# First loads in another order, stores between stages and later loads of q and v on GpSimd's queue: attention and two feed-forward layers, fp32

## The chip, the core and the metric

One core of a Trainium2 chip. The metric is the device time in microseconds of one execution, the median of several runs. One further execution was taken with the hardware profiler; every row below is from that one.

## What is computed

Linear attention over 4 batches of 8 heads (576 rows, 64 columns each), then two feed-forward layers over 2304 tokens, 512 wide, 2048 hidden, fp32:

```
q_s = softmax(q, last axis);  k_s = softmax(k, over the rows)
kv  = k_s^T v;  x = q_s kv                     (per batch and head)
h   = x @ w_in;   x2  = (h * sigmoid(1.702 h)) @ w_out
h2  = x2 @ w_in2; out = (h2 * tanh(softplus(h2))) @ w_out2
```

The weights arrive as float64 and are read as pairs of 32-bit words.

## The kernel before

Every fp32 operand of a large product is split into a high and a low fp32r part, and a product is three matmuls: high by high, high by low, low by high. Tokens run in five blocks of 512, 512, 512, 384 and 384. For the first three, layer 1 is computed chunk by chunk of the hidden width (48 steps n): twelve matmuls of L959 (h = x w_in), the activation on ScalarE and VectorE, and, two steps later, twelve of L1028 into four accumulators. The tokens of the last two blocks go through layer 1, and all of layer 2 follows, in a Strassen form with seven products in place of eight (L1250, L1480, L1589).

Weights come in 32 tiles of 512 KB per layer. Each is loaded into one of four `raw` buffers, turned from float64 into fp32 by ScalarE (L398, L362) and VectorE (L409, L422, L366), and split into high and low (L352, L353, L345). Layer 1's tiles stay in SBUF as `wi` and `wo`; sums and differences of them for the Strassen form, and layer 2's, are computed along the way and stored to a DRAM area (`combos` for w_in, `outs` for w_out), from which later stages load them into `wi`. x2 between the layers goes through DRAM too (`x2d`), and the attention output of the last two blocks (`xd`). The stores come from `store` (L446, called by `keep` and `combine1`), `combine` (L528), `right_parts` (L1391), `x2_evac` (L1080), `x_part` (L871); the loads that read them back from `ring_load` and `x_load`.

Attention is computed block by block between the matmuls of layer 1. Block 0's q goes to `qr`, its k and v to `kt` and `vd` or `gt`, at the start of the program. For the later blocks `q_load` (L754) fills `qt` with four or eight loads per half, `v_load` (L581) fills `vt` with two loads per pair of heads, `k_load` (L568) fills `kt`. For block 1 these loads have no condition of their own except that their tile is free; for the blocks behind it they wait for a step of layer 1.

All operations are recorded first, and a planner (`Plan`, L20 to L190) orders them: a list scheduler that simulates each engine as a queue, with a cost for every operation. All DMAs are one engine, `DMA`, whose cost is size / 305 ns times a factor `slow`, at least 650 ns; it adds 1400 ns from an engine to a DMA and 1050 back. An elementwise operation recorded with `either` (L341) may go to VectorE or to GpSimd; `SPARE` is what the planner adds to the finish time of either before it compares them. The program is then written out in the planned order, so each engine runs its own operations in that order and waits on semaphores for the others. In the kernel before every DMA is issued by SyncE, in the planned order.

Of the kernel before, what the change touches and what calls it, by code (L numbers as in the profile page):

```python
# [19 lines left out]
class Plan:  # L20
# [6 lines left out]
    SPARE = {DVE: 700.0, POOL: 2000.0}  # L27
# [183 lines left out]
def tile_attention_moe_moe(  # L211
# [107 lines left out]
    def f32(t):  # L319
        return t.bitcast(F32)  # L320
# [13 lines left out]
    def dma(size, reads, writes, out, in_, slow=1):  # L334
        plan.op(
            [(DMA, max(size * slow / 305.0, 650.0), lambda: nc.sync.dma_start(out=out(), in_=in_()), False)],
            reads,
            writes,
        )
# [41 lines left out]
    def decoded(m, io, fc, ri, di, pace=[], signed=True):  # L381
# [10 lines left out]
        dma(P * 4096, pace, [rl, rh], lambda: dst, lambda: src)  # L392
# [53 lines left out]
    def store(n, keys, j, u, out, in_):  # L446
        dma(P * n * 4, keys, [("combo", j, u)], out, in_)
# [80 lines left out]
    def combine(j, keys):  # L528
# [21 lines left out]
        for u, (n, ri, src, keys) in enumerate(parts):  # L550
            t = raw[ri].bitcast(F32R)
            hk, lk = [("raw", ri, 0)], [("raw", ri, 1)]
            split(n, lambda t=t, n=n: t[:, 0:n], lambda t=t, n=n: t[:, n : 2 * n], src, keys, hk, lk)
            dma(
                P * n * 8,
                hk + lk,
                [("combo", NFC // 2 + j, u)],
                lambda u=u, n=n: combos[NFC // 2 + j][:, u * 1024 : u * 1024 + 2 * n],
                lambda t=t, n=n: f32(t[:, 0 : 2 * n]),
            )  # L560
# [7 lines left out]
    def k_load(u, begun):  # L568
# [6 lines left out]
            lambda: k[b, 2 * hp : 2 * hp + 2].rearrange("h (p c) d -> p h c d", c=KC),  # L575
        )
# [4 lines left out]
    def v_load(u, begun):  # L581
        b, hp = divmod(u, NHP)
        if b == 0:
# [5 lines left out]
                lambda: v[b, 2 * hp : 2 * hp + 2].rearrange("h (p c) d -> p h (c d)", c=KC),  # L589
            )  # L590
            return
        for j in range(2):
# [6 lines left out]
                slow=2,  # L599
            )  # L600
# [153 lines left out]
    def q_load(blk, half, begun):  # L754
        cuts = q_cuts(blk)
        for i, (lo, hi) in enumerate(cuts):
            b, s = divmod(BASE[blk] + lo, S)
            for j in range(4):
# [6 lines left out]
                    slow=2,  # L765
                )
        return q_keys(range(4))

    def q_soft(blk, half, begun):
# [5 lines left out]
        if blk == 0:  # L775
# [6 lines left out]
                lambda: q[0, 4 * half : 4 * half + 4, 0 : SIZES[0], :].rearrange("h (p c) d -> p h c d", c=NCT),  # L782
            )
# [87 lines left out]
    def x_part(blk, hp, ps, key, i):  # L871
# [11 lines left out]
        if blk >= NDIR:  # L883
            t, keys = stage[hp % 3][:, 0:nb], [("stage", hp % 3)]
            from_psum(n, lambda: part(t), part(ps[:, 0:nb]), [key], keys)
            if i == len(q_cuts(blk)) - 1:
                to = (blk - NDIR) * NB
                dma(P * nb * 4, keys, [("xd", blk, hp)], lambda: xd[:, hp, to : to + nb], lambda: t)
# [191 lines left out]
    def x2_evac(blk):  # L1080
# [4 lines left out]
        for dm in range(NCC):  # L1085
# [5 lines left out]
            dma(P * nb * 4, keys, [("x2d", blk, dm)], lambda dm=dm: x2d[:, dm, BASE[blk] : BASE[blk + 1]], t)  # L1091
# [299 lines left out]
    def right_parts(j, base, keys, signed):  # L1391
# [24 lines left out]
        dma(P * 2048, rk[1][:1], [("outs", 0, j, a) for a in range(2)], lambda: outs[0][:, j], lambda: halved(f32(two[:, 0:512])))  # L1416
        stores = [(1, a, f32(one[:, a * 512 : a * 512 + 512]), rk[0][a : a + 1]) for a in range(2)]
        stores += [(3, 0, f32(hi[0]), rk[1][1:]), (3, 1, a0, [d0, ("ob", 0, 1)]), (5, 0, f32(hi[1]), mk), (5, 1, a1, [d1, ("ob", 1, 1)])]
        for i, a, src, keys in stores:
# [6 lines left out]
                slow=1.3,  # L1426
            )
# [338 lines left out]
```

## Time and profile before

| | us |
|---|---|
| median of 3 runs | 821.22 (818.87 to 823.44) |
| the profiled execution's own time | 823.01 |
| its span, from the first to the last instruction | 821.2 |
| PE busy | 809.6 (99%) |
| VectorE busy | 659.4 (80%) |
| ScalarE busy | 455.8 (56%) |
| GpSimd busy | 17.3 (2%) |

207.7 MB move by DMA in that time, and the packets took 76.7% of 16 DMA engines' span. The busy share of PE is no measure of its pace, since matmuls are pipelined; what it waited for and the granted clock are read from rows.

### The profile page before, as it was taken

The page shows a single profiled execution, that of the slowest core. Times are in us where ns is not written, and L with a number is a line of the kernel's source. Part 1 is how long each engine was busy: PE and PEld are TensorE (multiplying, and loading weights), DVE is VectorE, ACT ScalarE, POOL GpSimd, SP SyncE. Part 2 cuts the span into 40 slices and gives each one's busy share as a digit, 9 for nine tenths or more (in the row PEclk, how much of TensorE's full clock was granted, in tenths as well). Part 3 has the DMA queues.
Part 4 walks back from the last instruction along what each step waited for, and adds up shares of the span by engine and source line. Part 5 has one row for each costly group of instructions (what it writes and reads, how often), then busy time and mean ns, then how long its engine had stood idle before and what let it go on. Part 6 is the DMA issues. An engine that isn't in the chain of part 4 may idle for free.

```text
span 821.2 us, 14388 instructions
## 1 busy us (share of the span) xinstructions
PE 809.6 (99%) x5102; PEld 735.8 (90%) x5102; DVE 659.4 (80%) x1277; ACT 455.8 (56%) x915; POOL 17.3 (2%) x22
## 2 busy tenths in 40 slices
PE   8999899999999999999999999999999999999998
PEld 7788677877778887999999999999999999999998
DVE  6999897888976689866789879978777969777964
ACT  5989675445765555745457644555344554344542
POOL 0000000000000000000000000000000005000000
PEclk9999899999999999999999999999999999999999
DMA  9789556555688699878878897979588887778862
GB/s 258 213 251 306 187 182 187 207 154 168 195 264 283 225 300 313 257 279 285 327 269 275 319 320 251 341 284 406 188 263 293 291 293 253 226 261 259 270 197 59
DMA packets 126983, 208.57 MB, mean 254 GB/s; under 512 B 37568, under 2 KB 87488, under 8 KB 126912
## 3 DMA queue, kind: packets, MB, share of 16 engines
q1 hardware_dynamic: 126912, 207.66, 76.7%
q8 instruction: 41, 0.67, 0.3%
q14 instruction: 30, 0.25, 0.1%
HBM read 152.57 MB, written 55.05 MB: 253 GB/s over the span
## 4 chain that ended last, share of the span: by engine, by line
PE 61%; DMA 2%; DVE 1%; ACT 0%; issue 0%; ACTq 0%; SPq 0%
PE acc L1480 22%; PE at L1250 18%; PE h L1250 10%; PE acc L1589 5%; PE h L1589 3%; PE acc L1028 2%; DMA raw<-in_moe_w_in_dram 1%; DMA combos<-raw 1%; PE h L959 1%; PE h L1480 0%; DVE raw L345 0%; PE at L878 0%; PE at L848 0%; DVE dec L345 0%; DVE dec L422 0%
## 5 line engine op out<-in xcount | busy, mean ns | idle before, releaser
L959 PE MATMUL h<-xt,wi 128*128 128x512 f32 x576 | 149.0, 402 | 0.2 <-DVE xt L838 0.2
L1028 PE MATMUL acc<-g,wo 128*128 128x512 f32 x576 | 147.5, 398 | 0.0
L1480 PE MATMUL acc<-wi,second 128*128 128x256 f32 x1116 | 137.5, 283 | 0.0
L1480 PEld LDWEIGHTS acc<-wi,second 128*128 128x128 f32 x1116 | 135.6, 192 | 0.0
L959 PEld LDWEIGHTS h<-xt,wi 128*128 128x128 f32 x576 | 107.4, 190 | 25.0 <-issue 1.5
L1028 PEld LDWEIGHTS acc<-g,wo 128*128 128x128 f32 x576 | 106.6, 189 | 22.7 <-issue 0.4
L1250 PE MATMUL at<-xt,wi 128*128 128x384 f32 x612 | 119.0, 335 | 0.1
L1250 PEld LDWEIGHTS at<-xt,wi 128*128 128x128 f32 x612 | 106.8, 188 | 2.8 <-DVE quad L1302 0.4
L1272 ACT ACTIVATE quad<-quad 128x384 f32<-128x384 f32 x96 | 50.3, 525 | 90.8 <-DVE quad L1302 89.8
L353 ACT ACTIVATE second<-quad 128x384 fp32r<-128x384 f32 x126 | 65.2, 523 | 49.1 <-PE acc L1480 44.9
L345 DVE TENSOR_TENSOR second<-quad,second 128x384 fp32r<-128x384 f32 x125 | 74.0, 596 | 19.6 <-ACT second L353 19.0
L1250 PE MATMUL h<-xt,wi 128*128 128x384 f32 x348 | 66.0, 334 | 0.0
L345 DVE TENSOR_TENSOR quad<-quad 128x384 f32<-128x384 f32 x96 | 53.1, 556 | 13.2 <-ACT quad L1272 11.5
L1250 PEld LDWEIGHTS h<-xt,wi 128*128 128x128 f32 x348 | 60.9, 188 | 0.0
L353 ACT ACTIVATE raw<-dec 128x512 fp32r<-128x512 f32 (+1 forms) x64 | 37.2, 599 | 25.2 <-DVE dec L345 15.8
L1250 PE MATMUL at<-wi,wi 128*128 128x384 f32 x246 | 48.3, 335 | 0.0
L1480 PE MATMUL acc<-wi,g 128*128 128x256 f32 x372 | 48.2, 283 | 0.0
L1480 PEld LDWEIGHTS acc<-wi,g 128*128 128x128 f32 x372 | 46.2, 192 | 0.0
L422 DVE CUSTOM_DVE_ANT_0 dec<-raw,dec 128x1024 uint16<-128x1024 uint16 x64 | 44.7, 700 | 1.3
L398 ACT ACTIVATE dec<-raw 128x512 f32<-128x512 f32 x60 | 39.8, 669 | 7.9 <-DMA raw<-in_moe_w_in_dram 7.6
L1250 PEld LDWEIGHTS at<-wi,wi 128*128 128x128 f32 x246 | 43.2, 188 | 0.9 <-ACT stage L822 0.2
L353 ACT ACTIVATE g<-gt 128x512 fp32r<-128x512 f32 (+1 forms) x41 | 25.7, 626 | 32.6 <-PE acc L1028 19.1
(184 smaller groups left out, 1170.7 us busy)
## 6 DMA issues: line engine op xcount, KB each, us to landing
wi<-combos SPq DMA_DIRECT2D x96, 512.0 KB, 5.4
wi<-outs SPq DMA_DIRECT2D x76, 512.0 KB, 5.6
raw<-in_moe_w_in_dram SPq DMA_DIRECT2D x32, 512.0 KB, 4.8
raw<-in_moe_w_out_dram SPq DMA_DIRECT2D x32, 512.0 KB, 5.1
combos<-raw SPq DMA_DIRECT2D x32, 512.0 KB, 3.3
outs<-raw SPq DMA_DIRECT2D x32, 256.0 KB, 2.7
wi<-combos SPq DMA_DIRECT2D x32, 256.0 KB, 4.9
combos<-raw SPq DMA_DIRECT2D x24, 256.0 KB, 2.9
```

The lines of the kernel that those rows point to most:

```text
L345: return lambda: engine.tensor_tensor(out=out(), in0=in0(), in1=in1(), op=op)
L353: (ACT, act_ns(n), lambda: nc.scalar.activation(out=out(), in_=in_(), func=AF.Copy), False),
L398: lambda: nc.scalar.activation(out=f32(a), in_=f32(hi_w), func=AF.Prelu, scale=2.0**-112, alpha=2.0**32),
L422: dve(512, [rl], [da], lambda: nc.vector.tensor_tensor(out=a, in0=a, in1=lo_w, op=ALU.add), pair=True)
L959: nc.tensor.matmul(out=h(), lhsT=w_mm(fc, 0, a, cc), rhs=x_of(t)[:, cc, b, :], start=cc == 0 and i == 0, stop=cc == NCC - 1 and i == 2,)
L1028: nc.tensor.matmul(out=acc[dm][:, 0:nb], lhsT=w_mm(fc, 1, a, dm), rhs=g_of(n)[:, b, :], start=fc == 0 and i == 0, stop=fc == NFC - 1 and i ...
L1250: nc.tensor.matmul(out=bank_of(key)[:, 0:NB], lhsT=wt(fc, 0)[:, w : w + P], rhs=operand(k, b)[:, cc, :], start=cc == 0 and i == 0, stop=cc ...
L1272: nc.scalar.activation(out=t(), in_=t(), func=AF.Mish if n >= NPR else AF.Gelu_apprx_sigmoid)
L1480: nc.tensor.matmul(out=bank_of(banks[c])[:, at_ : at_ + 256], lhsT=slot(pr, a)[:, c * P : c * P + P], rhs=rhs(b), start=pr == 0 and i == 0 ...
L1589: nc.tensor.matmul(out=o, lhsT=w_mm(2 * n + j, 1, a, dm), rhs=g_tile(n, j)[:, b, lo:hi], start=n == 0 and j == 0 and i == 0 and (c < 4 or ...
```

## The change

- The planner never gives an elementwise operation to GpSimd (`SPARE` for it is 1e9).
- `dma` takes a queue. SyncE keeps the loads of weights, of k, of block 0's q and v, the loads back from DRAM, the stores of `gemm_out1` and of the result. GpSimd issues the stores to `combos`, `outs` and `xd`, the stores to `x2d` in `x2_evac`, and the loads of q and v for blocks 1 to 4. For the planner all of them are still the one engine `DMA`.
- The planner counts the loads of w_in tiles, of k, and of block 0's q and v 1.2 times as long.

```diff
--- before.py
+++ after.py
@@ -24,7 +24,7 @@
     WINDOW = 30.0
-    SPARE = {DVE: 700.0, POOL: 2000.0}
+    SPARE = {DVE: 700.0, POOL: 1e9}
     PASSES = 6
     IDLE = 110.0
     TICK = 3413.0
@@ -331,9 +331,9 @@
     def pe(ns, reads, writes, fn, whole=False):
         plan.op([(PE, ns, fn, whole)], reads, writes)
-    def dma(size, reads, writes, out, in_, slow=1):
+    def dma(size, reads, writes, out, in_, slow=1, queue=nc.sync):
         plan.op(
-            [(DMA, max(size * slow / 305.0, 650.0), lambda: nc.sync.dma_start(out=out(), in_=in_()), False)],
+            [(DMA, max(size * slow / 305.0, 650.0), lambda: queue.dma_start(out=out(), in_=in_()), False)],
             reads,
             writes,
         )
@@ -389,7 +389,7 @@
         else:
             dst = r
             src = w_ap[m][1][fc * P : (fc + 1) * P, :]
-        dma(P * 4096, pace, [rl, rh], lambda: dst, lambda: src)
+        dma(P * 4096, pace, [rl, rh], lambda: dst, lambda: src, slow=1.2 if io == 0 else 1)
         if signed:
             act(
                 512,
@@ -444,7 +444,7 @@
     stage = [st[:, i, :] for i in range(3)]
     def store(n, keys, j, u, out, in_):
-        dma(P * n * 4, keys, [("combo", j, u)], out, in_)
+        dma(P * n * 4, keys, [("combo", j, u)], out, in_, queue=nc.gpsimd)
     def halves(a):
         return a.rearrange("p (a q f) -> p a q f", a=2, q=2)
@@ -557,6 +557,7 @@
                 [("combo", NFC // 2 + j, u)],
                 lambda u=u, n=n: combos[NFC // 2 + j][:, u * 1024 : u * 1024 + 2 * n],
                 lambda t=t, n=n: f32(t[:, 0 : 2 * n]),
+                queue=nc.gpsimd,
             )
     def w_mm(fc, io, part, c, n=P):
@@ -573,6 +574,7 @@
             [("kt", k_tile(u))],
             lambda: kt[k_tile(u)],
             lambda: k[b, 2 * hp : 2 * hp + 2].rearrange("h (p c) d -> p h c d", c=KC),
+            slow=1.2,
         )
     def v_keys(u):
@@ -587,6 +589,7 @@
                 v_keys(u),
                 lambda: vd[u].rearrange("p j c d -> p j (c d)"),
                 lambda: v[b, 2 * hp : 2 * hp + 2].rearrange("h (p c) d -> p h (c d)", c=KC),
+                slow=1.2,
             )
             return
         for j in range(2):
@@ -597,6 +600,7 @@
                 lambda j=j: vt[:, j, :, 0:D],
                 lambda j=j: v[b, 2 * hp + j].rearrange("(p c) d -> p c d", c=KC),
                 slow=2,
+                queue=nc.gpsimd,
             )
     def k_max(u, ps, key):
@@ -763,6 +767,7 @@
                     lambda j=j, lo=lo, hi=hi: qt[lo // NCT : hi // NCT, :, j, :],
                     lambda j=j, b=b, s=s, n=hi - lo: q[b, 4 * half + j, s : s + n, :].rearrange("(p c) d -> p c d", c=NCT),
                     slow=2,
+                    queue=nc.gpsimd,
                 )
         return q_keys(range(4))
@@ -780,6 +785,7 @@
                 key,
                 lambda: qr[half],
                 lambda: q[0, 4 * half : 4 * half + 4, 0 : SIZES[0], :].rearrange("h (p c) d -> p h c d", c=NCT),
+                slow=1.2,
             )
             flat = lambda: qr[half].rearrange("p h c d -> p (h c) d")
         else:
@@ -885,7 +891,7 @@
             from_psum(n, lambda: part(t), part(ps[:, 0:nb]), [key], keys)
             if i == len(q_cuts(blk)) - 1:
                 to = (blk - NDIR) * NB
-                dma(P * nb * 4, keys, [("xd", blk, hp)], lambda: xd[:, hp, to : to + nb], lambda: t)
+                dma(P * nb * 4, keys, [("xd", blk, hp)], lambda: xd[:, hp, to : to + nb], lambda: t, queue=nc.gpsimd)
             return
         x = x_of(blk)
         hi_lo(
@@ -1088,7 +1094,7 @@
             if blk == NDIR - 1:
                 t, keys = lambda i=dm % 3: ob[i][:, 0:nb], [("dec", dm % 3), ("ob", dm % 3, 1)]
             from_psum(nb, t, acc[dm][:, 0:nb], [("acc", dm)], keys, scale=0.5)
-            dma(P * nb * 4, keys, [("x2d", blk, dm)], lambda dm=dm: x2d[:, dm, BASE[blk] : BASE[blk + 1]], t)
+            dma(P * nb * 4, keys, [("x2d", blk, dm)], lambda dm=dm: x2d[:, dm, BASE[blk] : BASE[blk + 1]], t, queue=nc.gpsimd)
@@ -1413,7 +1419,7 @@
             split(
                 512, lambda k=k: hi[k], lambda k=k: dec[k].bitcast(F32R)[:, :], lambda a=a: a, [d], hk, [d, ("ob", k, 1)]
             )
-        dma(P * 2048, rk[1][:1], [("outs", 0, j, a) for a in range(2)], lambda: outs[0][:, j], lambda: halved(f32(two[:, 0:512])))
+        dma(P * 2048, rk[1][:1], [("outs", 0, j, a) for a in range(2)], lambda: outs[0][:, j], lambda: halved(f32(two[:, 0:512])), queue=nc.gpsimd)
         stores = [(1, a, f32(one[:, a * 512 : a * 512 + 512]), rk[0][a : a + 1]) for a in range(2)]
         stores += [(3, 0, f32(hi[0]), rk[1][1:]), (3, 1, a0, [d0, ("ob", 0, 1)]), (5, 0, f32(hi[1]), mk), (5, 1, a1, [d1, ("ob", 1, 1)])]
         for i, a, src, keys in stores:
@@ -1424,6 +1430,7 @@
                 lambda i=i, a=a: outs[i : i + 2, :, j, a, :].rearrange("m p f -> p m f"),
                 lambda src=src: halved(src),
                 slow=1.3,
+                queue=nc.gpsimd,
             )
     def halved(a):
```

## Rows read from the trace of the kernel before

**Rows 1.** Waits of PE: who waited for whom, us in total, times, longest

```profile
PE at L878 <- ACT qT L858: 3.2, 1, 3.2
...
PE acc L638 <- DMA kt<-in_k_dram: 1.2, 1, 1.2
```

**Rows 2.** Busy time by stretch; PE, PEld, DVE, ACT, POOL (instructions), granted clock, DMA share, GB/s

```profile
84.00:88.00 4.00, 0.82 (x4) 0.39 (x4) 3.98 (x8) 3.07 (x6) 0.00 (x0) 0.85 0.85 277
88.00:92.00 4.00, 4.00 (x11) 3.08 (x11) 3.30 (x7) 2.09 (x5) 0.00 (x0) 0.50 0.65 191
...
100.00:120.00 20.00, 20.00 (x151) 15.62 (x148) 19.45 (x48) 14.61 (x52) 0.00 (x0) 1.00 0.52 167
...
180.00:220.00 40.00, 39.59 (x265) 31.21 (x264) 37.03 (x78) 24.70 (x49) 2.02 (x2) 1.00 0.57 162
220.00:260.00 40.00, 39.44 (x240) 31.18 (x239) 30.66 (x63) 25.04 (x51) 0.00 (x0) 1.00 0.82 276
...
475.00:757.00 282.00, 282.00 (x1939) 282.00 (x1939) 223.30 (x416) 132.52 (x260) 11.40 (x7) 1.00 0.83 280
```

**Rows 3.** Timeline of PE: start us, us, what [idle before <-releaser]

```profile
88.06 4.19 PE L959 MATMUL h<-xt,wi 128*128 128x512 f32 x9
...
112.07 2.31 PE L959 MATMUL h<-xt,wi 128*128 128x512 f32 x9
```

**Rows 4.** Timeline of all engines, 75 to 87 us, and L409's durations in ns

```profile
75.63 0.68 DVE L422 CUSTOM_DVE_ANT_0 dec<-raw,dec 128x1024 uint16<-128x1024 uint16 x1
...
77.80 1.63 POOL L345 TENSOR_TENSOR wi<-dec,wi 128x512 fp32r<-128x512 f32 x1 [75.91 <-ACT wi L353]
...
78.35 1.63 DVE L422 CUSTOM_DVE_ANT_0 dec<-raw,dec 128x1024 uint16<-128x1024 uint16 x1
...
80.04 0.34 SPq L336 DMA_DIRECT2D raw<-in_moe_w_out_dram  x1
...
85.85 0.67 ACT L362 ACTIVATE raw<-raw 128x512 int32<-128x512 uint32 x1 [0.61 <-DMA raw<-in_moe_w_out_dram]
...
86.97 0.59 ACT L858 ACTIVATE qT<-at 128x512 f32<-128x512 f32 x1
L409 DVE TENSOR_SCALAR dec<-dec x64: 406/418/429, 20.9 to 500.0; 128x512 int32<-128x512 int32 x64
```

**Rows 5.** Timeline of SyncE's queue and of PE in the head

```profile
0.73 0.45 SPq L336 DMA_DIRECT2D qr<-in_q_dram  x1
...
13.82 0.74 SPq L336 DMA_DIRECT2D vt<-in_v_dram  x1
26.11 0.93 PE L959 MATMUL h<-xt,wi 128*128 128x512 f32 x3
```

**Rows 6.** DMA issues: tile, KB each, median us from issue to landing

```profile
combos<-raw SPq DMA_DIRECT2D x32, 512.0 KB, 3.3
...
qt<-in_q_dram SPq DMA_DIRECT2D x8, 16.0 KB, 3.4
```

**Rows 7.** Timelines of ScalarE, PE and VectorE, 312 to 326 us

```profile
312.25 0.66 ACT L398 ACTIVATE dec<-raw 128x512 f32<-128x512 f32 x1 [1.15 <-DMA raw<-in_moe_w_in_dram]
314.30 0.85 PE L848 MATMUL at<-ident,qt 96*128 96x96 f32 x8 [0.69 <-ACT gt L982]
325.88 0.96 DVE L345 TENSOR_TENSOR raw<-wi,raw 128x768 f32<-128x768 f32 x1 [0.47 <-DMA wi<-xd]
```

**Rows 8.** Issues of q loads (ns min/median/max) and the maxima over q

```profile
L336 SPq DMA_DIRECT2D qt<-in_q_dram x21: 560/598/1287, 169.3 to 214.9; - x21
99.72 1.21 DVE L789 TENSOR_REDUCE qs<-qt 128x16 f32<-128x1024 f32 x1
...
179.29 1.21 DVE L789 TENSOR_REDUCE qs<-qt 128x16 f32<-128x1024 f32 x1
...
220.48 1.21 DVE L789 TENSOR_REDUCE qs<-qt 96x16 f32<-96x1024 f32 x1
```

## Prediction

> **What bounds the kernel now.** I read TensorE's waits first, because the chain of waits ends on PE almost everywhere. The two waits for other work that stand out are 3.2 us in front of the attention matmul at L878 and 1.2 us for the first k [rows 1]. Then the table by stretches: from 100 us on PE is busy through nearly every stretch at full granted clock: 20.00 of 20.00, 39.59 and 39.44 of 40.00, 282.00 of 282.00 from 475 to 757 us [rows 2]. In that part of the kernel hardly anything but a new stall can move the end. What is left to win lies in three places. (a) The head: the first matmul of layer 1 starts at 26.11 us [rows 5]. (b) A hole at 84 us: PE is busy 0.82 of 4.00 us, and the granted clock is 0.85 in that stretch and 0.50 in the next, against 1.00 from 100 us on [rows 2]; 0.50 is the 1.2 GHz level, reached after PE had idled. (c) Short waits after 100 us: 0.41 us in 180 to 220, 0.56 in 220 to 260 [rows 2], 0.69 at 314 [rows 7].
>
> The hole costs more than its wait. Nine matmuls of L959 took 4.19 us behind it and 2.31 elsewhere [rows 3]: 1.9 us of slow clock on top of 3.2 us of idling, 5.1 us together.
>
> Why the hole is there: a GpSimd subtraction (L345) runs from 77.80 to 79.43 us, and the VectorE step L422 that starts beside it takes 1.63 us, where it took 0.68 at 75.63. SyncE could issue the next load of a weight tile only behind it, at 80.04; ScalarE's L362 starts 0.61 us late at 85.85 because of that load, and the copy qT (L858), for which PE waits, comes two places behind it at 86.97 [rows 4].
>
> **The change, part by part.** *No elementwise work on GpSimd.* Eleven subtractions and additions go back to VectorE. The one at 77.80 us costs VectorE an operation more, which I estimate at the 0.68 us of L422 on the same tile, and gives back 1.63 - 0.68 = 0.95 [rows 4], so it is a gain of 0.3 us of VectorE and 0.95 us at the load that waited. Seven others lie between 475 and 757 us, where VectorE idles 282.0 - 223.3 = 58.7 us and PE never waits [rows 2]: zero there. Without that cover it would be some 0.6 us each, 4 us for the seven. For the hole I take -0.95 us; the ends are 0 (VectorE and ScalarE are as full as before and the wait moves elsewhere) and -5.1 us (the wait ends before PE needs the data, and the clock does not fall).
>
> *Another order of the first loads.* The planner is told that k, v, blk-0 q and all w_in tiles take 1.2 times as long. No byte changes, only which transfer is put where. PE's wait for the first k is 1.2 us, and 512 KB of q are issued first, at 0.73 us [rows 1, 5]. If k goes first, the head could win these 1.2 us. Against it stands a side effect of the queue: the load of v for the next batch (vt, 144 KB) is issued at 13.82 us now only because it stands behind fifteen others on SyncE, of which the first stands here [rows 5]. It waits for nothing; on GpSimd's own queue it can start as soon as GpSimd has set the constants, and goes ahead of loads that the head needs. Both halves are 288 KB; at the 277 GB/s of 84 to 88 us that is 1.0 us of all DMA engines [rows 2]. I take 0, with ends -1.2 and +1.0. The same factor on the w_in tiles re-plans everything behind it; in stretches where PE has no gap this can only do nothing or harm.
>
> *Stores issued by GpSimd.* 228 transfers move: 72 into combos, 56 into outs, 12 into x2d, 8 into xd, 24 of v, 56 of q, counted from the groups of the issue table, of which the first and the last stand here [rows 6]. The stores are read back by loads that still go through SyncE and wait for the landing, so order is kept by semaphores, not by the queue. What SyncE saves is its issue time, and it costs nothing today: it is on no row of PE's waits. What a store can cost is its buffer: raw and dec tiles are decoded into again when it has landed, and ScalarE and VectorE, which work in order, stand still if the load behind it is late. One such chain is in the trace: ScalarE waits 1.15 us for a w_in tile at 312.25 and PE then 0.69 us [rows 7]; so about half a microsecond is hidden there and the rest reaches PE. The tightest store is xd, whose read-back VectorE waits 0.47 us for at 325.88 [rows 7]. No row shows a store issued by GpSimd. Bounds: a gain of at most the 0.69 us above, if stores no longer delay loads; a loss of one SyncE issue, 0.4 us, per chain and some fifteen chains, 6 us, if nothing hides them. I take 0, between the two and at the row where such a chain was partly hidden.
>
> *Later loads of q and v issued by GpSimd.* A group of eight q loads stands ahead of each softmax half; SyncE needs 0.598 us for the median issue and up to 1.287 [rows 8]. VectorE starts its maximum at 179.29, right where the last of the group of 169 to 177 us lands: no slack in the plan. If GpSimd needs x us per load, the group lands 8 (x - 0.6) later, and VectorE stands still for it with everything queued behind: the activation's subtraction, the weight decodes, the next k. PE feels it when VectorE's idle time is used up. Four groups are used soon after their last issue; their maxima start at 99.72, 179.29, 202 and 220.48 (the first, the second and the last stand here [rows 8]). The idle time that follows them is 0.55 us in 100 to 120, 2.97 in 180 to 220 for two of them, and 9.34 in 220 to 260 [rows 2]. At x = 0.6 the cost is 0; at 1.0 (3.2 us per group) 2.65 + 3.4 + 0 = 6.1 us; at 1.29 (5.5 us) 4.95 + 8.0 + 0 = 13 us. I take 0, the end that lies at a measured row; in favour of it is that those loads no longer stand behind a raw load that waits for its buffer.
>
> Sum: 0 (head) - 0.95 (hole) + 0 + 0 = -0.95 us on a span of 821.24. The profiled execution's own time is 823.01, 1.8 us over the median 821.22; set against the median, 820.3 us.
>
> **A rule against this change.** The trace shows that GpSimd and VectorE hold each other up: 1.63 us for a step of 0.68 beside a GpSimd operation [rows 4]. The Trainium skill, "SBUF — State Buffer", section "SBUF: two separate sides", says that a DMA issued by GpSimd has its descriptors written by GpSimd's cores, which a VectorE operation in a two-port mode locks out, and advises SyncE's or ScalarE's queue for it. No run so far shows this for a DMA. By that rule the third rival below would happen; by the rows alone it may not.
>
> **The rivals.**
>
> 1. *The hole closes, and the head gains.* For it: the load that came late was late by a GpSimd operation that is gone, and no q load or store stands before it on SyncE. Against it: VectorE is busy 3.98 of 4.00 us in 84 to 88 [rows 2], so its work, not one load, may be what is late. Time: 821.2 - 5.1 - 1.2 = 814.9.
>
> 2. *Slower: GpSimd issues q and v loads at a slower pace.* Place: the softmax halves between 85 and 330 us. For it: nothing in the plan knows that GpSimd is another queue with another pace, and the plan has no slack at 179 us. Against it: VectorE idles elsewhere, and a short stop of it need not reach PE, as at 312 us [rows 7]. It decides from about 0.9 us per load, where the sum passes 4 us; at 1.0 it gives 827, at 1.29 834.
>
> 3. *Slower: each GpSimd issue waits for a VectorE operation.* The shift L409 takes 0.42 us and is there 64 times [rows 4]; one such step in front of every load of a group makes 0.6 + 0.42 = 1.02 us per load, so 827 by the same sum, and seven stores of a right_parts step land 7 x 0.42 = 2.9 us late, of which PE sees what is over the cover of half a microsecond to several. Against it: such short steps fill only a part of VectorE's time.
>
> 4. *It does not do what it says:* the loads and stores leave GpSimd as they left SyncE, and only the new plan counts: 819 to 823, the forecast's own case.
>
> **How the numbers follow.** Within 0.5% (817.1 to 825.3; about what a measurement of this kernel can tell from no change): 0.38, with 820.3 as its time; rival 4 is in it. Rival 1 and partial versions of it that pass -4.1 us: 0.34. Rival 2: 0.18, rival 3: 0.10, together 0.28 for slower. The range reaches to rival 1 with a little more for a shorter head, 812, and to the upper price of rival 2, 834; I leave 0.08 under and 0.10 over. The forecast's own range is 817 to 825.
>
> **What would show it.** Right: PE's wait at L878 near 84 us shrinks by about 1 us or goes with the clock's dip; L422 has no 1.63 us row; the first L959 stays near 26 us; PE busy stays full from 100 us. For rival 1: no stretch under 1.00 of granted clock after 30 us. For rival 2: the queue of GpSimd shows over 0.9 us per q load, and VectorE's waits name qt or vt with several microseconds. For rival 3: issues on GpSimd that last long only where L409, L366 or a copy of VectorE runs. The prediction is wrong if PE gains idle time after 100 us, or if the head moves by more than 1.2 us.

## The result, and the profile after

The change makes the kernel slower: 830.84 us (828.56 to 831.65) against 820.42 (818.87 to 823.44), a ratio of 1.0118 with a 95% interval of 1.0081 to 1.0155. The forecast was 820.3, with 817 to 825 as its own range: no change.

What the forecast hoped for at 84 us did happen. Waits of PE in the changed kernel (who waited for whom: us in total, times, longest), to be read against [rows 1]; line numbers are 4 to 7 higher than before:

```profile
PE at L1256 <- ACT xt L353: 2.8, 1, 2.8
...
PE acc L1596 <- ACT dec L828: 1.1, 1, 1.1
PE at L884 <- ACT qT L864: 1.1, 2, 0.7
...
PE acc L642 <- DMA kt<-in_k_dram: 0.5, 1, 0.5
```

And the stretches, in the columns of [rows 2], with the durations of L422 (ns min/median/max):

```profile
84.00:88.00 4.00, 4.00 (x21) 3.31 (x20) 3.82 (x9) 2.96 (x7) 1.92 (x3) 1.00 0.96 286
...
330.00:475.00 145.00, 139.99 (x771) 129.08 (x770) 104.35 (x207) 80.73 (x150) 30.83 (x47) 0.98 0.80 277
L422 DVE CUSTOM_DVE_ANT_0 dec<-raw,dec x64: 676/686/695, 22.6 to 517.2; 128x1024 uint16<-128x1024 uint16 x64
```

The hole is gone: PE is busy 4.00 of 4.00 us at a granted clock of 1.00, and no L422 is longer than 0.695 us where one took 1.63 [rows 4]. The largest part of the loss stands in a stretch that had none: from 330 to 475 us PE was busy 144.93 of 145.00 us before and is 139.99 now, and PE waits at L1256 for a copy of ScalarE. The same stretch of the kernel before:

```profile
330.00:475.00 145.00, 144.93 (x821) 134.73 (x821) 115.70 (x228) 85.00 (x159) 0.00 (x0) 1.00 0.84 288
```

Most of what follows compares when PE's lines begin, since the program on PE is the same in the changed kernel and in most of the experiments. First the changed kernel, then the same plan with every DMA on SyncE (the first experiment); the two numbers behind the durations are the first and the last start in us:

```profile
L965 PE MATMUL h<-xt,wi x576: 387/389/792, 25.4 to 325.2; 128*128 128x512 f32 x192
L1256 PE MATMUL at<-xt,wi x612: 333/334/689, 328.1 to 763.6; 128*128 128x384 f32 x153
L1487 PE MATMUL acc<-wi,second x1116: 278/283/283, 528.4 to 822.6; 128*128 128x256 f32 x186
```

```profile
L965 PE MATMUL h<-xt,wi x576: 387/389/792, 24.4 to 321.0; 128*128 128x512 f32 x192
L1256 PE MATMUL at<-xt,wi x612: 333/334/445, 324.0 to 751.6; 128*128 128x384 f32 x153
L1487 PE MATMUL acc<-wi,second x1116: 278/283/283, 516.5 to 810.6; 128*128 128x256 f32 x186
```

I call the part up to the first L965 the head, from there to the first L1256 the attention stage, and from there to the first L1487 the middle; what comes after, to the last start of L1487 in the group shown, takes 294 to 295 us in every run. Against SyncE alone the change loses 1.0 us in the head, 302.7 - 299.6 = 3.1 in the attention stage and 200.3 - 192.5 = 7.8 in the middle, together 11.9; the spans differ by 11.8 (829.9 and 818.1). The profiled execution of the kernel before (823.01 us) lay 2.2 to 3.3 us above the medians of its later runs, so stages are compared with SyncE alone.

DMA queues (packets, MB, share of 16 engines' span) and the loads of v (KB each, median us from issue to landing) of the changed kernel, one line of GpSimd's issues for [rows 8], and the stores outs<-dec issued from 340 to 470 us:

```profile
q1 hardware_dynamic: 66944, 151.67, 55.6%
q0 software_dynamic: 17984, 55.98, 19.4%
...
vt<-in_v_dram POOLq DMA_DIRECT2D x24, 144.0 KB, 4.8
L336 POOL DMA_DIRECT2D qt<-in_q_dram x56: 512/592/867, 23.1 to 298.1; - x56
outs<-dec POOLq DMA_DIRECT2D x15, 256.0 KB, 5.4
```

The loads of v and these stores with SyncE alone:

```profile
vt<-in_v_dram SPq DMA_DIRECT2D x24, 144.0 KB, 3.7
outs<-dec SPq DMA_DIRECT2D x12, 256.0 KB, 5.3
```

A q load costs GpSimd 0.592 us where SyncE needed 0.598. What is later over the whole run is the landing: 4.8 us for v (3.7 with SyncE alone), 4.1 for outs<-raw (3.0) and 5.0 for outs<-dec (4.6). But from 340 to 470 us, where most is lost, outs<-dec lands in 5.4 us against 5.3 with SyncE alone: a later median landing of these stores does not explain the loss there; which transfer is late has to be looked up.

### The profile page after: what moved, and what is told of

Read it like the earlier page. It is cut to its first block, busy times and chain, and to the rows that moved or that the text cites. A ratio compares the mean times of both kernels' runs of the same rounds, so it can differ in the third digit from the quotient of the medians.

```text
span 829.9 us, 14508 instructions
## 1 busy us (share of the span) xinstructions
PE 813.0 (98%) x5109; PEld 736.8 (89%) x5109; DVE 652.3 (79%) x1279; ACT 460.8 (56%) x924; POOL 149.1 (18%) x239
## 3 DMA queue, kind: packets, MB, share of 16 engines
q1 hardware_dynamic: 66944, 151.67, 55.6%
q0 software_dynamic: 17984, 55.98, 19.4%
## 4 chain that ended last, share of the span: by engine, by line
PE 43%; DMA 3%; DVE 2%; issue 2%; ACT 0%; POOL 0%; SPq 0%; DVEq 0%; ACTq 0%; POOLq 0%
PE acc L1487 22%; PE at L1256 11%; PE h L1256 9%; DMA wi<-combos 1%; PE acc L1596 1%; DMA raw<-in_moe_w_out_dram 1%; DMA combos<-raw 1%; DVE dec L345 1%; DVE raw L345 0%; PE h L1487 0%; PE h L1596 0%; DVE xt L345 0%; DVE stage L1308 0%; POOL outs L336 0%; DVE gt L1308 0%
## 5 line engine op out<-in xcount | busy, mean ns | idle before, releaser
L965 PE MATMUL h<-xt,wi 128*128 128x512 f32 x576 | 146.8, 398 | 0.8 <-DVE xt L844 0.6
L1487 PE MATMUL acc<-wi,second 128*128 128x256 f32 x1116 | 137.5, 283 | 0.0
L1487 PEld LDWEIGHTS acc<-wi,second 128*128 128x128 f32 x1116 | 135.6, 192 | 0.0
L965 PEld LDWEIGHTS h<-xt,wi 128*128 128x128 f32 x576 | 106.4, 188 | 25.5 <-issue 1.2
L1034 PEld LDWEIGHTS acc<-g,wo 128*128 128x128 f32 x576 | 105.9, 188 | 24.7 <-ACT stage L828 2.3
L1256 PE MATMUL at<-xt,wi 128*128 128x384 f32 x612 | 120.9, 338 | 4.9 <-ACT xt L353 2.8
L1256 PEld LDWEIGHTS at<-xt,wi 128*128 128x128 f32 x612 | 107.2, 189 | 9.1 <-ACT xt L353 3.0
L345 DVE TENSOR_TENSOR second<-quad,second 128x384 fp32r<-128x384 f32 x126 | 69.2, 554 | 19.0 <-ACT second L353 18.6
L1256 PE MATMUL h<-xt,wi 128*128 128x384 f32 x348 | 66.0, 334 | 0.0
L1256 PEld LDWEIGHTS h<-xt,wi 128*128 128x128 f32 x348 | 60.8, 188 | 0.0
L336 POOL DMA_DIRECT2D combos<-raw x56 | 33.5, 600 | 100.9 <-DVE raw L345 92.7
L336 POOL DMA_DIRECT2D qt<-in_q_dram x56 | 35.3, 636 | 85.5 <-PE at L854 60.7
L1256 PE MATMUL at<-wi,wi 128*128 128x384 f32 x246 | 49.1, 339 | 0.0
L1487 PE MATMUL acc<-wi,g 128*128 128x256 f32 x372 | 48.2, 283 | 0.0
L988 ACT ACTIVATE gt<-h 128x512 f32<-128x512 f32 x41 | 24.3, 592 | 41.2 <-PE h L965 41.2
L1487 PEld LDWEIGHTS acc<-wi,g 128*128 128x128 f32 x372 | 46.2, 192 | 0.0
```

The source lines that it names most:

```text
L336: [(DMA, max(size * slow / 305.0, 650.0), lambda: queue.dma_start(out=out(), in_=in_()), False)],
L345: return lambda: engine.tensor_tensor(out=out(), in0=in0(), in1=in1(), op=op)
L965: nc.tensor.matmul(out=h(), lhsT=w_mm(fc, 0, a, cc), rhs=x_of(t)[:, cc, b, :], start=cc == 0 and i == 0, stop=cc == NCC - 1 and i == 2,)
L988: act(nb, [hk, ("tables",)], [tk], lambda: nc.scalar.activation(out=t, in_=h, func=AF.Tanh, scale=0.851), psum=True)
L1034: nc.tensor.matmul(out=acc[dm][:, 0:nb], lhsT=w_mm(fc, 1, a, dm), rhs=g_of(n)[:, b, :], start=fc == 0 and i == 0, stop=fc == NFC - 1 and i ...
L1256: nc.tensor.matmul(out=bank_of(key)[:, 0:NB], lhsT=wt(fc, 0)[:, w : w + P], rhs=operand(k, b)[:, cc, :], start=cc == 0 and i == 0, stop=cc ...
```

## The experiments

Unless said otherwise each is the changed kernel with one thing altered, so that the orders on PE, VectorE and ScalarE are those of the change. Times are medians, and each ratio is to runs of the kernel before made along with it (their medians lie between 819.7 and 820.8 us). What an experiment costs is counted against SyncE alone. Head, attention and middle come from one profiled execution of each kernel, which lies up to 2.6 us from the kernel's median, so a difference of that size between two stages shows little by itself.

| run | us | ratio to before (95%) | head | attention | middle |
|---|---|---|---|---|---|
| the kernel before | 820.42 | | 26.1 | 303.2 | 190.3 |
| the change | 830.84 | 1.0081 to 1.0155 | 25.4 | 302.7 | 200.3 |
| all on SyncE | 820.51 | 0.9986 to 1.0023 | 24.4 | 299.6 | 192.5 |
| old plan, queues of the change | 837.92 | 1.0189 to 1.0248 | 26.7 | 309.4 | 197.6 |
| stores on GpSimd | 834.15 | 1.0154 to 1.0208 | 24.4 | 308.1 | 199.3 |
| q and v loads on GpSimd | 826.72 | 1.0057 to 1.0127 | 25.7 | 304.0 | 192.4 |
| all on GpSimd | 830.31 | 1.0076 to 1.0155 | 25.5 | 304.0 | 194.2 |
| plan told of 1 us more | 841.33 | 1.0215 to 1.0292 | 25.4 | 311.0 | 204.3 |
| outs stores on GpSimd | 824.23 | 1.0033 to 1.0081 | 24.4 | 300.2 | 198.5 |
| combos stores on GpSimd | 834.34 | 1.0129 to 1.0199 | 24.5 | 308.7 | 197.2 |
| reloads on GpSimd too | 836.16 | 1.0162 to 1.0225 | 24.4 | 304.0 | 202.8 |
| before, no GpSimd elementwise | 820.47 | 0.9983 to 1.0020 | 28.0 | 296.8 | 193.1 |
| before, factor 1.2 | 826.02 | 1.0045 to 1.0094 | 25.2 | 303.6 | 194.9 |
| q loads on GpSimd | 822.79 | 1.0002 to 1.0045 | 24.8 | 303.1 | 192.5 |
| SyncE from 328 us on | 824.70 | 1.0029 to 1.0065 | 24.7 | 302.2 | 192.7 |

**Queues or plan.** All DMAs of the change on SyncE, and the opposite, the queues of the change under the plan of before:

```diff
-lambda: queue.dma_start(...)
+lambda: nc.sync.dma_start(...)
```

> The changed kernel's order on TensorE, VectorE and ScalarE, unchanged, with every DMA issued by SyncE again. Theory Q (the loss comes from stores that land later when GpSimd issues them: dec to outs 5.4 us at the median of 340 to 470 us against 3.3 before): about 821 us, PE without the 2.8 us wait at 457 us. Rival P (the loss comes from the new order, made by the 1.2 factor and by GpSimd's ban on elementwise work): 829 to 832 us, the wait at 457 us still there.

```diff
-    SPARE = {DVE: 700.0, POOL: 1e9}
+    SPARE = {DVE: 700.0, POOL: 2000.0}
...
-slow=1.2
```

> The order of the kernel before, with the changed kernel's queues: stores between stages and later q and v loads issued by GpSimd, which also still does its eleven elementwise operations. Theory Q: 826 to 832 us, with PE waits at the first x_split of layer 2 near 455 us. Rival P: within 2 us of the kernel before, since the order is the old one.

Measured 820.51 and 837.92; the second lies above theory Q's range. The new plan alone is worth nothing that can be measured; the queues cost 10 us under the new plan and 18 under the old. The loss is the queues'.

**Which of the moved transfers.** Four kernels with `queue=nc.sync` put back at the other places:

> The changed kernel with only the q and v loads given back to SyncE. Theory Q: as slow as the changed kernel, 829 to 832 us, since the stores are what lands late. Prediction's rival 2 (late q and v loads): 821 to 824 us. Rival P: 829 to 832 us.

> The changed kernel with only the stores given back to SyncE; GpSimd issues just the later q and v loads. Theory Q: about 821 us. Rival 2: 829 us or more. Rival P: 829 to 832 us, like the changed kernel.

> The changed plan, and of all moved DMAs only the stores to outs in right_parts issued by GpSimd (56 of them, from 328 us on); all else on SyncE. If the stall at 454 us comes from the chain outs<-dec, decode, raw, combos<-raw that starts with these stores, the most of what the stores cost shows here: 825 to 831 us, with all of it behind 330 us. If the later landing of any one class has slack and only several together use it up, 819 to 823.

> The changed plan, and only the stores to combos (72) issued by GpSimd, all else on SyncE. By the chain of the stall at 454 us their own landing is its last link (5.26 us for combos<-raw before the DVE split): 822 to 826 us if a later landing costs at that link alone, 819 to 822 if the outs stores make the loss, above 828 if the combos stores make it. Together with the run with outs alone it says whether the parts add.

The stores alone cost 13.6 us, the loads 6.2, both 10.3: they do not add, and neither run lies in the range that theory Q or rival 2 gave for it. The outs stores alone cost 3.7 us, just under the 825 us expected of them, and lose in the middle (198.5 us against 192.5). With the combos stores alone (13.8) most of the loss is in the attention stage, 9.1 us, where the whole change loses 3.1. The trace of the run with the stores alone, which has the same longest wait of PE at L884 (4.7 us), says why. Its GpSimd queue at 62 us; the landing of w_in tiles issued in 62 to 70 us, first with SyncE alone, then here; then ScalarE and PE:

```profile
61.98 2.43 POOL L336 DMA_DIRECT2D combos<-wi  x4 [7.88 <-DVE wi L345]
```

```profile
raw<-in_moe_w_in_dram SPq DMA_DIRECT2D x2, 512.0 KB, 4.9
```

```profile
raw<-in_moe_w_in_dram SPq DMA_DIRECT2D x2, 512.0 KB, 7.9
83.50 0.65 ACT L362 ACTIVATE raw<-raw 128x512 int32<-128x512 uint32 x1 [2.30 <-DMA raw<-in_moe_w_in_dram]
PE at L884 <- ACT qT L864: 5.4, 2, 4.7
```

Four stores go out at 62 us as soon as their data is there; on SyncE two of them stood at 76.47 and five at 96.31, behind weight loads. The weights land 3 us later and PE waits 4.7 us in the place of the old hole; the mean granted clock is 0.79 from 84 to 88 us. In the change itself q loads that wait for PE stand in front of these stores on GpSimd's queue, which issues nothing between 37.8 and 81.75 us, and nothing of this happens. An empty queue lets a transfer run ahead of the plan; by these traces that was the harm here, but no run tests it by itself.

**One queue, but GpSimd's.**

```diff
-lambda: queue.dma_start(...)
+lambda: nc.gpsimd.dma_start(...)
```

> The changed plan, with every DMA on GpSimd's queue, so that there is again one queue in the planned order, as with every DMA on SyncE (820.5 us), but issued by GpSimd. Theory R (run ahead): what costs is that with two queues SyncE's loads no longer stand behind the stores of GpSimd, start earlier and take the transfer engines from them; with one queue that can't happen, so 819 to 823 us, and the stores land as early as with SyncE alone (outs<-dec 4.6, outs<-raw 3.0 us). Theory G (each transfer that GpSimd issues starts later, whoever stands beside it): at least the 830.8 us of the change, rather 835 to 850, since the loads of weights are late now too (raw<-w_in above 5.2 us to landing, 4.7 with SyncE).

830.31, half a microsecond under the least that theory G asked. The landings and the stages split the verdict: outs<-dec lands in 4.6 us, as theory R asked, and outs<-raw in 3.9, which is later; the w_in tiles take 4.8 us and not the more than 5.2 of theory G. The middle takes 194.2 us, 1.7 more than with SyncE alone and 6.1 less than with two queues; the head and the attention stage lose 5.5. A GpSimd queue that holds everything keeps most of the middle; two queues lose it.

**Telling the planner.** GpSimd's transfers counted 1.0 us later, as `late` in the planner's delays:

```diff
+                    d += 1000.0 if (i if ways else b) in self.late else 0.0
```

> The change, queues as in it, and the planner told that what GpSimd loads or stores is there 1.0 us later (the excess of the medians to landing over those with SyncE alone is between 0.3 and 2.6 us, most near 1.0). If the loss is spacing that the plan didn't know of, most of the 11 us returns: 819 to 824 us, and PE's waits on ScalarE's xt behind 454 us go. If the buffers leave no room for a longer landing (raw and dec are held until the store has landed), 828 to 833 us, as the change.

841.33, worse than the change and above both ranges; the waits moved (PE 4.9 us for ScalarE's stage, 3.7 for its dec). Counting a fixed 1 us did not help. The new plan also reorders everything, so this says no more.

**Where the middle is lost.** In the changed kernel, SyncE's and GpSimd's queues and who waits, 428 to 462 us, in order of time:

```profile
428.39 6.48 SPq L336 DMA_DIRECT2D wi<-combos  x7
436.60 2.13 POOL L336 DMA_DIRECT2D outs<-dec  x3 [14.38 <-DVE dec L345]
441.17 0.66 ACT L398 ACTIVATE dec<-raw 128x512 f32<-128x512 f32 x1 [2.92 <-DMA outs<-dec]
448.11 1.19 POOL L336 DMA_DIRECT2D combos<-raw  x2 [9.38 <-DVE raw L345]
453.39 0.96 DVE L345 TENSOR_TENSOR raw<-wi,wi 128x768 f32<-128x768 f32 x1 [1.27 <-DMA combos<-raw]
457.02 0.44 PE L1256 MATMUL at<-xt,wi 128*128 128x384 f32 x1 [2.79 <-ACT xt L353]
460.12 2.12 PE L1256 MATMUL at<-wi,wi 128*128 128x384 f32 x6
464.51 1.20 PE L1256 MATMUL at<-wi,wi 128*128 128x384 f32 x6
```

The same transfers with SyncE alone:

```profile
424.71 0.92 SPq L336 DMA_DIRECT2D wi<-combos  x2
431.87 1.42 SPq L336 DMA_DIRECT2D outs<-dec  x3
433.39 2.61 SPq L336 DMA_DIRECT2D wi<-combos  x5
...
434.12 0.68 ACT L398 ACTIVATE dec<-raw 128x512 f32<-128x512 f32 x1 [0.36 <-DMA outs<-dec]
```

On one queue the plan put two reloads in front of the three outs stores and five behind them. On two queues SyncE does not stand in front of the stores until VectorE has their data; it issues seven reloads first. The stores then land in 4.4 us (the median of that stretch) where they took 2.5, ScalarE waits 2.92 us for a dec tile where it waited 0.36, and by way of the next decode, its store and the split, PE waits 2.79 us at 457, and behind it six matmuls take 2.12 us where six of the same line take 1.20 at 464 us; the mean granted clock from 455 to 465 us, behind that wait, is 0.66, and 1.00 with SyncE alone. PE's waits in the middle come to 6.0 us against 1.3 with SyncE alone, and the matmuls from 457.02 to 464.51 us take 2.7 us longer than the same ones there: together 7.4 of the 7.8 us. Two experiments on this:

```diff
 # ring_load: both dma(...)
+                queue=nc.gpsimd,
```

> The change, with the loads that read combos and outs back (wi<-combos, wi<-outs, in ring_load) moved to GpSimd's queue too, so that they stand behind the stores in the planned order again; weights and k stay on SyncE. Theory R (order between the queues is lost: SyncE's reloads run ahead of the stores, as the seven wi<-combos that one trace issued from 426 us, where with one queue two go then and five behind outs<-dec at 433): the stretch from the first L1256 to the first L1487, 200.3 us in the change, 192.5 with all on SyncE and 194.2 with all on GpSimd, comes down to 193 to 196, and the time to 823 to 827 us. Theory G (later landing of what GpSimd issues, whoever stands beside it): more transfers land late, the stretch stays at 199 or above and the time is 830 to 840 us.

```diff
+    stores_on[0] = nc.sync      # behind the loop over n < NS
```

> The change, but what GpSimd would issue behind the steps of layer 1 (recorded after the loop over n below NS) is issued by SyncE: two queues until about 328 us, one from there. If the loss of the middle stretch comes from two queues there (200.3 us against 192.5), that stretch is 192 to 194 us and the time 822 to 824.5 us, the rest being the 3 to 5 us of the attention. If it comes from stores that were late before 328 us, the stretch stays above 197 and the time above 827.

SyncE from 328 us on settles the place: the middle is back at 192.7 us, as expected if two queues there make the loss, and the time is 824.70, 0.2 over the range. The first starts that give the 192.7 (PE's lines are 3 higher here):

```profile
L1259 PE MATMUL at<-xt,wi x612: 332/335/446, 326.9 to 754.8; 128*128 128x384 f32 x153
L1490 PE MATMUL acc<-wi,second x1116: 279/284/284, 519.6 to 813.8; 128*128 128x256 f32 x186
```

Moving the reloads to GpSimd did not do what theory R asked: 202.8 us for the middle and 836.16 in all, which by the numbers written down is theory G's case. Against theory G stands the run with all on GpSimd, whose middle takes 194.2 us though every transfer is GpSimd's. The trace with the reloads moved: GpSimd's and SyncE's queue, then ScalarE, and for comparison the two lines of all on GpSimd:

```profile
427.87 1.12 POOL L336 DMA_DIRECT2D wi<-combos  x2
428.76 0.33 SPq L336 DMA_DIRECT2D raw<-in_moe_w_out_dram  x1
429.19 3.19 SPq L336 DMA_DIRECT2D raw<-in_moe_w_in_dram  x2
436.66 0.67 ACT L398 ACTIVATE dec<-raw 128x512 f32<-128x512 f32 x1 [5.46 <-DMA raw<-in_moe_w_out_dram]
```

```profile
431.52 0.76 POOL L336 DMA_DIRECT2D raw<-in_moe_w_in_dram  x1 [3.74 <-DMA combos<-raw]
432.27 1.09 POOL L336 DMA_DIRECT2D wi<-combos  x2
```

Now stores and reloads kept their order, and another pair lost it: the two reloads go ahead of the w_out tile issued at 428.76 and of the two w_in tiles, behind all of which they stand on one queue. The w_out tile takes 7.8 us; ScalarE waits 5.46 us for it, VectorE for ScalarE, and PE 2.75 us at 440.66. The theory had the wrong pair for a cause: by this trace any transfers on two queues can lose their order, not stores and reloads alone. That two queues make the loss of the middle is shown by the runs; that it is the lost order which does it is read from the traces, and from the transfers by themselves below.

**Transfers by themselves.** Four kernels time a load or store of 512 KB, alone or with up to four bulk loads of 512 KB released at the same time by one VectorE operation. In the first its cases ran beside one another, so it tells nothing.

> Not the attention kernel: it computes nothing of the reference and only times transfers, each case eight times, with a wait for everything between. A load of 512 KB (w_out's tile) or a store of 512 KB, issued by SyncE or GpSimd: alone; followed at once by four bulk loads of 512 KB on the same queue; or by four on the other queue; and alone beside 14 VectorE additions. Theory G (GpSimd's transfers land late by themselves): alone on GpSimd 0.7 us or more later than alone on SyncE (the excess of combos<-raw, outs<-raw and wi<-combos with all on GpSimd is 0.7 to 0.9), and the bulk's queue matters by under 0.5 us. Theory S (two queues share the transfer engines, so what is urgent no longer goes first): alone within 0.5 us of each other; in front of four bulk loads of the same queue within 1 us of alone; with the four on the other queue 2 us later or more, up to all five ending together. The VectorE lock (the prediction's rival 3): GpSimd's alone lands at least 0.4 us later beside the additions, SyncE's does not.

> The same transfers, now one case after the other, the bulk loads from w_in so that they can be told from the urgent one (a load of w_out or a store), and as before nothing of the reference computed. Theory G (GpSimd's transfers land late by themselves): alone on GpSimd 0.7 us or more later than alone on SyncE, for loads and stores, and which queue the bulk stands on matters by under 0.5 us. Theory S (two queues share the transfer engines): alone within 0.5 us of each other; in front of four bulk loads of the same queue within 1 us of alone; with the four on the other queue 2 us later or more. The VectorE lock: GpSimd's alone lands at least 0.4 us later beside the additions, SyncE's does not.

> Transfers by themselves again, nothing of the reference computed. Alone a GpSimd load of 512 KB landed in 3.6 us and a SyncE one in 3.2; with four bulk loads issued at the same time by SyncE the GpSimd load took 6.6 us and a store 7.4, while SyncE's beside GpSimd's bulk stayed at 3.2. Now the number of bulk loads is 1, 2 or 4, and either the bulk or the urgent transfer comes two VectorE operations (some 1.4 us) later. Theory first come, first served (GpSimd's transfer merely reaches the engines 0.4 us later, and so behind the bulk): bulk 1.4 us later leaves GpSimd's at 3.6 to 4.2 us; an urgent transfer 1.4 us behind the bulk lands late on either queue, SyncE's beside GpSimd's bulk as well (5.5 us or more with four); with one or two bulk loads the excess is one or two loads of some 1.3 us. Theory rank (SyncE's queue goes before GpSimd's whenever both have work): GpSimd's lands at 6 us or more even where the bulk comes 1.4 us later, and SyncE's stays below 4.2 us even behind GpSimd's bulk.

> Transfers by themselves, nothing of the reference computed: a load or a store of 512 KB by SyncE or by GpSimd, alone and beside twenty VectorE multiplications of one operand by a constant (the kind of L409, 0.42 us each, issued back to back), sixteen times each. The prediction's rival 3 (a GpSimd issue waits for the VectorE operation): beside them GpSimd's land 0.4 us later or more than the 3.6 and 2.9 us alone, up to 8 us if the twenty leave no gap; SyncE's stay at 3.2 and 2.6. Without such a lock all four stay within 0.2 us of alone, as they did beside additions of two operands (3.6 and 3.2).

The second, in pairs of SyncE and GpSimd: a load alone (xa, xb), a store alone (sinkg, sinkh); a load and a store with the bulk on the other queue (xd, xe; sinkj, sinkk); and the first two bulk loads and the urgent load of xe, in order of time:

```profile
xa<-in_moe_w_out_dram SPq DMA_DIRECT2D x8, 512.0 KB, 3.2
xb<-in_moe_w_out_dram POOLq DMA_DIRECT2D x8, 512.0 KB, 3.6
...
xd<-in_moe_w_out_dram SPq DMA_DIRECT2D x8, 512.0 KB, 3.2
xe<-in_moe_w_out_dram POOLq DMA_DIRECT2D x8, 512.0 KB, 6.6
sinkg<-xg SPq DMA_DIRECT2D x8, 512.0 KB, 2.6
sinkh<-xh POOLq DMA_DIRECT2D x8, 512.0 KB, 2.9
...
sinkj<-xj SPq DMA_DIRECT2D x8, 512.0 KB, 2.7
sinkk<-xk POOLq DMA_DIRECT2D x8, 512.0 KB, 7.4
221.50 0.80 SPq L58 DMA_DIRECT2D xe<-in_moe_w_in_dram  x2
221.77 0.53 POOL L56 DMA_DIRECT2D xe<-in_moe_w_out_dram  x1 [8.26 <-DVE xe L52]
```

The third: GpSimd's load beside one and two bulk loads of SyncE (xa, xb), beside four that come 1.4 us later (xd), and SyncE's urgent load 1.4 us behind four bulk loads of GpSimd (xh; behind four of SyncE it took 7.4 us):

```profile
xa<-in_moe_w_out_dram POOLq DMA_DIRECT2D x8, 512.0 KB, 5.1
xb<-in_moe_w_out_dram POOLq DMA_DIRECT2D x8, 512.0 KB, 6.5
...
xd<-in_moe_w_out_dram POOLq DMA_DIRECT2D x8, 512.0 KB, 3.6
...
xh<-in_moe_w_out_dram SPq DMA_DIRECT2D x8, 512.0 KB, 6.6
```

By itself GpSimd's transfer lands 0.2 to 0.4 us later, less than theory G wanted. Beside SyncE's bulk it lands 3.0 to 4.5 us later, while SyncE's beside GpSimd's bulk loses nothing: theory S asked for a loss on both, so it holds by half. The third kernel says why: with the bulk 1.4 us later GpSimd's load is back at 3.6 us, and SyncE's, 1.4 us behind GpSimd's bulk, is late too. In these cases what comes first goes first, and of two transfers released in the same moment GpSimd's comes second: in the rows shown its issue begins 0.27 us after SyncE's first and takes 0.53 us, and by its end, at 222.30 us, SyncE has issued two bulk loads. This fits that four bulk loads (6.6 us) delay it no more than two (6.5); the store took 7.3 us beside two and 7.4 beside four. The Trainium skill, "DMA: Bandwidth & Descriptors", section "Latency and other measured facts", gives some 0.6 us to the first byte for SyncE's path and 1 us for GpSimd's; the 0.4 us between the loads alone agree. The same page of the Trainium skill, section "SWDGE vs HWDGE vs iDMA", says that a transfer engine takes turns between its queues; by that, as an estimate, the excess would be that of one bulk load however many there are. With one (5.1 us) and two (6.5 us) it is not.

Beside twenty one-operand VectorE operations (the last kernel) GpSimd's load took 3.7 us against 3.5 alone and its store 3.0 against 2.9, SyncE's 3.2 and 2.6. The lock of which the Trainium skill, "SBUF — State Buffer", section "SBUF: two separate sides", cited in the prediction, speaks is worth 0.2 us at most here.

**Q alone, and the two parts of the plan.** These left only the loads of q on GpSimd, and applied one half of the plan's change to the kernel before, all on SyncE:

> The changed plan, stores and the loads of v on SyncE, only the 56 loads of q issued by GpSimd (with v as well: 826.7 us, all on SyncE: 820.5). If v's loads are the path (there PE waited 2.2 us at L718 for vt, landing 4.8 us against 3.7): 820 to 822.5 us, and the first L1256 near 324 to 325 us (329.7 with v, 324.0 without either). If q's are (qt 32 KB at 4.5 against 2.2, 112 KB at 4.8 against 3.7): 825 to 828.

> The kernel before with only the planner's price of GpSimd at 1e9, all DMAs on SyncE, loads in the order that this plan gives. The prediction's step (the hole at 84 us, where the 1.63 us decode beside a GpSimd operation stood, closes): 818.5 to 819.5 us, no L422 above 1 us, no wait of PE at L878 near 84 us. Rival: any change of a planner's cost reorders the whole list (half of the rows of each engine), and what it gains at 84 us is noise beside that: anywhere from 815 to 828 us.

> The kernel before with only the planner's 1.2 for the loads of w_in, k and block 0's q and v, all DMAs on SyncE, elementwise operations on GpSimd as before. The prediction priced the order of the first loads between a gain of 1.2 and a loss of 1.0: 818.8 to 821 us; with the one that leaves out GpSimd's elementwise work it must give what both together give (820.5) if the two parts add.

Q alone: 822.79, just over what was expected if v's loads were the path, but the first L1256 came at 327.9 and not at 324 to 325 us: 3.5 us of the 4.4 that q and v together cost in the attention stage are there already. So by the traces v is not the path alone; by the medians q alone costs 2.3 us and q with v 6.2. Without elementwise work on GpSimd: 820.47, nothing measurable, and outside the 818.5 to 819.5 expected; factor 1.2 alone: 826.02, 5 us slower, where 818.8 to 821 was expected. They do not add to the 820.51 of both.

## Why the prediction was wrong, step by step

*What bounds the kernel*: right, as far as it goes. PE was full from 100 us on, only a new stall could move the end, and a new stall did. The sign by which the prediction called itself wrong, idle time on PE after 100 us, is what came.

*No elementwise work on GpSimd, -0.95 us*: the mechanism is borne out in part, its gain did not arrive. The 1.63 us row is gone in the change and in both runs without that work on SyncE; in the run with this edit alone PE's wait fell from 3.2 to 1.7 us and the clock stayed at 1.00, but the wait did not go. In the run with factor 1.2 alone, where GpSimd keeps its elementwise work, that wait is 2.0 us and no L422 is longer than 0.695 us, so a new plan alone moves both as much. With this edit alone the attention stage is 6.4 us shorter than before's, the head 1.9 and the middle 2.8 us longer: the plan is made anew, and what one place gains others give back.

*Another order of the first loads, 0*: the first L965 went from 26.11 to 25.40 us and the wait for k from 1.2 to 0.5 us, inside the bounds; with SyncE alone it came at 24.4 us, half a microsecond beyond them. The early v load did not come: on GpSimd's queue it stands behind q loads that wait for PE, the first at 23.11 us, and was issued at 29.25. But the factor re-plans what lies behind, which the prediction said could only do nothing or harm and did not price; alone it costs 5 us, outside the ends of -1.2 and +1.0.

*Stores issued by GpSimd, 0 (at most +6)*: this step failed. It said that order is kept by semaphores, not by the queue. Semaphores keep a store before its own reload. What kept it before reloads that have nothing to do with it was SyncE standing in front of the store until its data was there, and the prediction counted of SyncE only its issue time, at nothing. That standing was the planner's order of transfers. The change took it away, and the middle alone lost 7.8 us, more than the 6 that the prediction allowed; with the stores of the middle back on SyncE, 0.2 us of that is left.

*Later loads of q and v, 0*: the pace I took, 0.6 us per load, is what was measured (0.592), and rival 2, a pace over 0.9 us, did not occur, though its time range, 827 to 834, holds the result: that is luck. This term failed too: the loads alone cost 6.2 us. The sum asked only how long an issue takes. It left out when a load lands (v 4.8 us at the median, 3.7 with SyncE alone; 512 KB by themselves 0.2 to 0.4 us later, and 1.5 to 3.0 beside SyncE's loads) and what goes ahead of it; which of the two cost the 6.2 us is not shown. Rival 3, a lock by VectorE, is 0.2 us at most.

*Rival 1* happened at 84 us and in part in the head (0.7 of its 1.2 us) and was overtaken; its sign, no granted clock under 1.00 after 30 us, fails with the 0.66 at 455 us. *Rival 4*, that only the plan counts, is the run with SyncE alone (820.51): it would have been right without the queues.

Open: how the 3.1 us of the attention stage divide between the later landing and the lost order (all on GpSimd loses 4.4 there with one queue); why the old plan suffers more, 18 us; and why the planner's extra 1 us made things worse.

## What to carry to other kernels

A queue that waits is also an order: before transfers are moved to a second queue, list which later ones stood behind them only because the issuer waited, since these now go first and share the engines. Move a transfer to GpSimd only if it may land a few tenths of a us later by itself and several us later when SyncE issues bulk loads at the same time. And a planned program should be compared with the new plan on the old queue, since re-planning alone moved this kernel by up to 5 us.

## What the runs showed of the hardware that was not expected

GpSimd's transfers go through a queue of their own (software_dynamic, 55.98 MB in 17984 packets) and took the transfer engines no longer per byte: 19.4% of their span for 55.98 MB, against 55.6% for 151.67. Which of two transfers comes first decided more than which queue it is on: released together, 0.4 us of delay became 3.0 for a load and 4.5 for a store; the excess of the load grew with one and two bulk loads (1.5 and 2.9 us) and no further with four (3.0), two being what SyncE had issued by the end of GpSimd's issue.
